# Chunk 0's gates ahead of the weight conversion, chunk 1's gates as a group, and filler products at a phase change, in a fused mLSTM and mixture-of-experts kernel

## Chip, core and metric

The kernel runs on one core of a Trainium2 chip. The metric is the device time in microseconds (us) of one execution; the runs before are given as the median of three. Five engines work side by side and meet through semaphores: PE multiplies matrices, ACT (ScalarE) evaluates functions and copies, DVE (VectorE) and POOL (GpSimd) do element-wise work, SP issues most transfers. Each engine takes its instructions in the order in which the program wrote them for it.

## What is computed

```
# 1. attention (mLSTM): 2 batches x 8 heads, 768 tokens, head size 40
for t in range(S):
    m_new = max(f_gate[t] + m, i_gate[t])
    f_stab, i_stab = exp(f_gate[t] + m - m_new), exp(i_gate[t] - m_new)
    C = f_stab * C + i_stab * outer(v_t, k_t);  n = f_stab * n + i_stab * k_t
    y[t] = sigmoid(o_gate[t]) * (C @ q_t) / max(abs(n . q_t), 1)
# 2. dense layer: 1536 tokens x 320, hidden 2048
x = softplus(x @ w_in) @ w_out
# 3. top-1 mixture: 8 experts, hidden 1024
e = argmax(x @ w_gate)
out = gate_w * sigmoid(x @ w_output_gate)[e] * (relu(x @ w1[e]) @ w2[e])
```

## The kernel before

The attention is done in 6 chunks (c) of 128 tokens for each of 2 batches (b). `gates` turns the gate inputs of some chunks into running sums: scans and small steps on DVE along the time axis (tiles mm, fg, acum, ig, scratch), transposes on PE (gps), exponentials on ACT and one negation on DVE (both into gts). Chunk 0 has a call of its own; chunks 1 to 5 share one, so their steps are 640 columns wide. A chunk then needs: the masked running sums on PE (ap), decays on ACT (abc<-ap, abc), scores on PE (sp), their product with the decays on DVE (abc<-sp,abc), the weighted values (pv), a state update (kv, cst), the part carried over from the chunk before (qc), and a division and sigmoid (num, sm, y, og). Its result is transposed (xp) and split into a high half (xh) and a rest (xl); where these two lie in the weights' tiles the trace names them win and wou.

The dense layer takes its weights from `w_in`, 16 pieces (n) that arrive as raw 64-bit words (wra); `conv` makes each a float (wta, three DVE steps), rounds it on ACT or DVE (win or wou) and subtracts the rounded part. Its products are ph (up), softplus on ACT and DVE (ab, g, gh, gl), and acc (down), in legs over ranges of pieces and blocks of 256 tokens.

Then the program passes to the experts. The last block's rows are routed (x2tp, lg, rsm, counts), the first four slots of tokens are put together on PE (xe), their halves written by ACT and DVE (flat<-xe), and the experts' products begin (ph<-w1s). `split_w2` rounds the eight experts' w2 on ACT (w2s<-w2raw) and `low_w2` subtracts the rounded part on POOL or DVE; the first down products (yp) wait for all eight. `warm` puts products of ones on PE that nothing reads.

The order of the work is set when the program is built. `Weaver` keeps a clock for each engine, prices every instruction (`Priced`), and always lets the task go on that can start earliest; the number given with `W.add` breaks ties. A `yield "V"` offers the next step to DVE (P is PE, A ACT, G POOL, S SP), a `yield [event]` holds the task back until the event has been signalled; these events steer only the order in which instructions are written down. The waits on the chip follow from the data. As every instruction is issued through one helper, the trace gives line 196 for nearly all of them, and tiles' names have to tell them apart.

Of the kernel before, what the change touches and what calls it, by code (L numbers as in the profile page):

```python
# [45 lines left out]
class Weaver:  # L46
# [4 lines left out]
    def __init__(self):  # L51
        self.clock = {e: 0.0 for e in "PAVGS"}
        self.tasks, self.cur, self.progress = [], None, 0.0
        self.last, self.at, self.dma = None, 0.0, 1.2
        self.columns = {}
        self.port = 0.0
        self.tick, self.hot = 0, False
# [92 lines left out]
class Priced:  # L150
# [3 lines left out]
    def __getattr__(self, name):  # L154
        fn = getattr(self.e, name)

        def call(*args, **kw):
# [19 lines left out]
            elif self.l == "V":  # L177
                wide = name in ("tensor_scalar", "tensor_copy", "memset") and not near and n not in (384, 768, 164)
                wide = wide or name == "tensor_scalar" and n in (384, 704)
                cost = 0.068 + n * (0.0065 if name == "reciprocal" else 0.00113 if "scan" in name else 0.00052 if wide  # L180
                                    else 0.00104)
                far = [t is None or t.space != PSUM for t in (src, kw.get("in1"))]
                port = all(far) and ("in1" in kw or wide)
            elif self.l == "G":
                port = not name.startswith("indirect") and n > 16
                cost = 1.04 if name.startswith("indirect") else 0.04 + n * 0.0008 if name in ("memset", "iota") else \
                    0.12 + n * (0.0033 if name == "tensor_copy" else 0.00092 if name == "affine_select" else
                                0.00175 if n in (320, 328, 164) else 0.0022)
            else:
                cost = 0.46  # L190
                run = 160 if out.shape[-1] == 40 else 512
                nbytes = out.shape[0] * n * 4 / (180e3 if run < 512 else 360e3)
# [42 lines left out]
def mlstm_moe_kernel(ctx: ExitStack, tc: tile.TileContext, q_t, k_t, k, v, i_gate, f_gate, o_gate,  # L235
# [72 lines left out]
    acum = moe.tile([GG, S], F32, tag="row1", name="acum")  # L308
    have_gates = Event(n=2)
    for r, t in x_ring.items():  # L310
        t.free[0] = (t.free[0][0], have_gates)
    read_acum, read_parts = Event(n=2), Event(n=2 + 2 * B * NSP)
    row_ring.free[0:3] = [(f"row{n}", ev) for n, ev in enumerate((have_gates, read_acum, read_parts))]
# [56 lines left out]

    gate_scan = Event()

    have_fi = Event()

    def load_gates():
        yield "S"
        SP.dma_start(fg, f_gate)
        SP.dma_start(ig, i_gate)
        W.signal(have_fi)

    def heat():
# [3 lines left out]
        for _ in range(HEAT):  # L385
            PE.matmul(warm, ones, ones.unsqueeze(1).to_broadcast([P, 2, P]), start=True, stop=True)
        W.signal(ev)

    def gates(n, c0, c1):
# [3 lines left out]
        if n:  # L393
            yield [gate_scan, have_g[0]]
        yield "V"
        DVE.tensor_tensor_scan(out=mm[:, t0:t1], data0=fg[:, t0:t1], data1=ig[:, t0:t1],
                               initial=NEG if n == 0 else mm[:, t0 - 1:t0], op0=ALU.add, op1=ALU.max)
        if n == 0:
            W.signal(gate_scan)
        yield "V"  # L400
# [140 lines left out]
    def chunk(b, c):  # L541
        if c > 1:
            yield [done_chunk[b][c - 2]]
        rank = 0 if c == 0 else 2 + 0.1 * c
        more = c < NCH - 1
# [77 lines left out]
        def carried():  # L623
            yield [done_c[b][c - 1], have_q[c]]
            box["num"] = num, _ = yield from work["num"].get([P, H, D1], F32, "num")
# [161 lines left out]
    def conv():  # L787
        for n in range(NF):
            W.cur.rank = RANKS[n]
            yield [have_raw[n]]  # L790
            raw, e1 = raws.pop(n)
# [111 lines left out]
    def route(blk, acc, full, part):  # L903
# [60 lines left out]
        for t in range(T2):  # L964
            ACT.activation(out=ex[:, t], in_=le[:, t], func=AF.Exp, bias=nmx[:, t:t + 1], accum_out=ssum[:, t:t + 1])
        ACT.activation(out=ef, in_=oge, func=AF.Exp, scale=-1.0)
        yield [Event(ranked), state[blk], have_rows]
        if final:
# [106 lines left out]

    have_room, up_done, have_turned = Event(), Event(), Event()
    have_last_lg, have_counts, have_chosen, have_parts, have_early = Event(), Event(), Event(), Event(n=TPB), Event()
# [301 lines left out]
    def split_w2(qn):  # L1379
# [5 lines left out]
        w2s = right["w2s"]  # L1385
        if qn == 0:
            yield [x_done]
        for e in range(E):
            yield [w2_raw[qn, e]] + ([begun[e + 2]] if qn == 0 else [])
            r, ev = w2_t.pop((qn, e))  # L1390
            yield "AV"
            copy(w2s[:, 0, :, e, :], r)
# [14 lines left out]
    def low_w2(qn, e, r, ev):  # L1407
        yield "VG"
        (psub if W.cur.on == "G" else vsub)(right["w2s"][:, 1, :, e, :], r, right["w2s"][:, 0, :, e, :].bitcast(F32))
# [6 lines left out]
    W.add(gates(0, 0, 1), 0)  # L1416
    W.add(gates(1, 1, NCH), 1)
    W.add(loads(0, 1), 1)
# [5 lines left out]
    for c in range(NCH):  # L1424
        for b in range(B):
            W.add(chunk(b, c), 0 if c == 0 else 2 + 0.1 * c)
    W.add(constants(), 5)
# [10 lines left out]
    def get_experts(s0, s1, ready, when):  # L1438
# [17 lines left out]
        evals.update(zip(range(s0, s1), vals))  # L1456
        W.signal(have_evals[s0])

    have_evals, have_meta = ({0: Event(), KNOWN: Event()} for _ in range(2))
# [10 lines left out]
    W.add(get_experts(KNOWN, NS, state[NBLK], rows_turned), 0)  # L1470
    W.add(turned_on(), 0)
    W.add(warm(turned_rows[0], 2), 0)
    W.add(warm(have_last_lg, 2), 0)
# [294 lines left out]
```

## Time and profile before

| what | value |
|---|---|
| median of three runs | 439.86 us (439.1 to 443.94) |
| profiled execution: device time / span from first to last instruction | 441.47 us / 439.8 us |
| PE busy / DVE busy / ACT busy / POOL busy, share of the span | 94% / 78% / 69% / 42% |
| mean granted TensorE clock | 0.97 of full speed |

The device time is 1.67 us over the span. A row of the timeline gives the start, the time busy, and in brackets how long the engine sat idle before it and what ended that. [...]

### The profile page before, as it was taken

Reading aid. Unit: us, or ns where it says so; the run is one execution under the profiler, and the core shown is the slowest. Engines: PE = TensorE matmul, PEld = TensorE weight load, DVE = VectorE, ACT = ScalarE, POOL = GpSimd, SP = SyncE. Lnnn points to the kernel's source line nnn. Section 1 sums busy time; section 2 is a strip of 40 time slices with the busy share of each in tenths; the row PEclk is TensorE's granted clock in tenths of the full one; section 3 lists DMA queues with packets and bytes.
Section 4 is the critical chain, followed back from the end, with each engine's and each line's share of the span. In section 5 each row is a group of like instructions: output and inputs, shape, how many; then the busy total and the mean of one; then the engine's idle time right before and its main releaser. Section 6 shows DMA issues by size and latency. Waiting matters only on the chain.

```text
span 439.8 us, 9798 instructions
## 1 busy us (share of the span) xinstructions
PE 414.8 (94%) x3073; PEld 394.0 (90%) x3073; DVE 344.0 (78%) x900; ACT 302.7 (69%) x877; POOL 182.7 (42%) x244
## 2 busy tenths in 40 slices
PE   8669999999999999999999999798999999999993
PEld 7657999999999999999999999677899898998893
DVE  3998999997998999997766656656954898798662
ACT  1559698978688887876967769417889675666230
POOL 5247585747120211130210102114766377387654
PEclk9896999999999999999999999969999999999998
DMA  8969659299347330132100101128636736644112
GB/s 266 334 199 305 207 150 279 91 299 318 132 121 290 107 103 30 32 91 60 38 11 28 38 1 38 57 87 254 204 124 179 253 105 221 202 133 147 41 66 78
DMA packets 32282, 62.88 MB, mean 143 GB/s; under 512 B 4218, under 2 KB 16765, under 8 KB 32230
## 3 DMA queue, kind: packets, MB, share of 16 engines
q1 hardware_dynamic: 30742, 57.87, 41.5%
q0 software_dynamic: 1488, 4.35, 2.7%
q8 instruction: 28, 0.46, 0.4%
q14 instruction: 24, 0.20, 0.2%
HBM read 54.05 MB, written 8.65 MB: 143 GB/s over the span
## 4 chain that ended last, share of the span: by engine, by line
PE 66%; DVE 11%; ACT 9%; DMA 8%; issue 3%; POOL 2%; SPq 1%; POOLq 0%; ACTq 0%; DVEq 0%
PE ph L196 26%; PE acc L196 17%; PE yp L196 11%; DMA out_dram<-yac,tki 3%; PE tp L196 2%; ACT abc L196 2%; PE lg L196 2%; DMA og<-in_o_gate_dram 2%; DVE wta L196 2%; PE sp L196 2%; DMA wra<-in_w_in_dram 2%; ACT ab L196 2%; PE pv L196 2%; DVE w2s L196 1%; DMA vn<-in_v_dram 1%
## 5 line engine op out<-in xcount | busy, mean ns | idle before, releaser
L196 ACT ACTIVATE ab<-ab 128x256 f32<-128x256 f32 x192 | 78.2, 416 | 2.9
L196 PE MATMUL ph<-w1s,flat 128*128 x312 | 59.6, 334 | 2.7 <-DVE hr L196 1.5
L196 POOL TENSOR_TENSOR w1s<-w1raw,w1s 64x256 fp32r<-64x256 f32 (+1 forms) x39 | 40.3, 1047 | 47.7 <-ACT w1s L196 23.9
L196 PE MATMUL acc<-win,gh 128*128 128x320 f32 x240 | 55.7, 317 | 0.0
L196 PE MATMUL yp<-w2s,hh 128*128 x240 | 54.5, 314 | 1.0 <-POOL w2s L196 0.9
L196 PEld LDWEIGHTS ph<-w1s,flat 128*128 128x128 f32 x312 | 46.6, 189 | 8.6 <-DVE hr L196 1.9
L196 DVE TENSOR_TENSOR gl<-g,gh 128x256 fp32r<-128x256 f32 x96 | 44.5, 467 | 12.3 <-ACT gh L196 11.2
L196 ACT ACTIVATE ab<-ph 128x256 f32<-128x256 f32 x96 | 36.3, 378 | 21.5 <-PE ph L196 20.9
L196 DVE SCALAR_TENSOR_TENSOR g<-ph,ab 128x256 f32<-128x256 f32 x96 | 39.9, 417 | 12.9 <-ACT ab L196 12.5
L196 POOL DMA_INDIRECT rows<-row,rsm x12 | 12.1, 1008 | 79.9 <-DVE rsm L196 25.9
L196 ACT CAST gh<-g 128x256 fp32r<-128x256 f32 x96 | 37.9, 397 | 8.9 <-DVE g L196 6.4
L196 POOL TENSOR_TENSOR w2s<-w2raw,w2s 128x640 fp32r<-128x640 f32 x20 | 35.8, 1811 | 17.3 <-ACT w2s L196 12.3
L196 PE MATMUL ph<-win 128*128 128x256 f32 x250 | 42.3, 289 | 0.0
L196 PEld LDWEIGHTS yp<-w2s,hh 128*128 128x128 f32 x240 | 39.7, 188 | 2.9 <-POOL w2s L196 1.1
L196 PEld LDWEIGHTS acc<-win,gh 128*128 128x128 f32 x240 | 38.7, 189 | 0.1
L196 DVE TENSOR_TENSOR hr<-ph,hr 128x256 f32<-128x256 f32 x60 | 24.5, 419 | 18.2 <-ACT hr L196 15.5
L196 PE MATMUL yp<-w2s,hl 128*128 x120 | 37.3, 311 | 0.0
L196 PE MATMUL acc<-win,gl 128*128 128x320 f32 x120 | 37.1, 309 | 0.0
L196 ACT COPY hr<-ph 128x256 f32<-128x256 f32 x60 | 22.8, 380 | 19.1 <-PE ph L196 18.5
L196 PEld LDWEIGHTS ph<-win 128*128 128x128 f32 x250 | 35.3, 193 | 0.0
L196 PE MATMUL acc<-wou,gh 128*128 128x320 f32 x144 | 33.2, 315 | 2.3 <-ACT gh L196 2.3
L196 ACT CAST w2s<-w2raw 128x640 fp32r<-128x640 f32 x32 | 23.3, 742 | 13.8 <-PE yp L196 13.8
(209 smaller groups left out, 1080.7 us busy)
## 6 DMA issues: line engine op xcount, KB each, us to landing
w1raw<-in_w_dram SPq DMA_DIRECT2D x32, 384.0 KB, 3.9
wra<-in_w_in_dram SPq DMA_DIRECT2D x16, 704.0 KB, 6.5
w2raw<-in_w_dram SPq DMA_DIRECT2D x32, 320.0 KB, 3.3
abc<-abc_dram SPq DMA_DIRECT2D x4, 1024.0 KB, 7.4
rows<-pad SPq DMA_DIRECT2D x19, 194.0 KB, 4.1
qT<-in_q_t_dram SPq DMA_DIRECT2D x6, 512.0 KB, 5.2
kn<-in_k_dram SPq DMA_DIRECT2D x5, 416.0 KB, 7.3
vn<-in_v_dram SPq DMA_DIRECT2D x6, 320.0 KB, 6.9
```

Source lines behind the costliest of these rows:

```text
L196: return fn(*args, **kw)
```

## The change

`conv` holds its first piece back until chunk 0's gates have been written down. The gates come as three groups: chunk 0, chunk 1, chunks 2 to 5. Chunk 1's attention gets rank 1.5 in place of 2.1, and its carried part waits, in the planner, for its gates. The planner's prices of a scan on DVE, of the first transfers and of the first products are altered. At the change of phase, five more products of ones are written behind the registers' load that follows the dense layer's last up product, the rounding of the first six w2 pieces is tied to the last block's exponentials (have_exps) and no longer to the first slots' halves (x_done), and in this first round rounding is offered to ACT alone and the subtraction to POOL alone.

```diff
@@ Weaver
-        self.last, self.at, self.dma = None, 0.0, 1.2
+        self.last, self.at, self.dma = None, 0.0, 2.4
@@ Priced
-                cost = 0.068 + n * (0.0065 if name == "reciprocal" else 0.00113 if "scan" in name else 0.00052 if wide
+                cost = 0.068 + n * (0.0065 if name == "reciprocal" else 0.0022 if "scan" in name else 0.00052 if wide
@@ load_gates, heat
         W.signal(have_fi)
+        W.dma += 0.9
...
+        W.clock["P"] = 8.1
         W.signal(ev)
@@ gates
         if n:
-            yield [gate_scan, have_g[0]]
+            yield [gate_scan[n - 1], have_g[n - 1]]
...
-        if n == 0:
-            W.signal(gate_scan)
+        if n < 2:
+            W.signal(gate_scan[n])
@@ chunk, carried
-        rank = 0 if c == 0 else 2 + 0.1 * c
+        rank = 0 if c == 0 else 1.5 if c == 1 else 2 + 0.1 * c
...
-            yield [done_c[b][c - 1], have_q[c]]
+            yield [done_c[b][c - 1], have_q[c], have_g[c]]
@@ conv
-            yield [have_raw[n]]
+            yield [have_raw[n]] + ([have_g[0]] if n == 0 else [])
@@ route
         ACT.activation(out=ef, in_=oge, func=AF.Exp, scale=-1.0)
+        if final:
+            W.signal(have_exps)
@@ split_w2
-        if qn == 0:
-            yield [x_done]
         for e in range(E):
-            yield [w2_raw[qn, e]] + ([begun[e + 2]] if qn == 0 else [])
+            yield [w2_raw[qn, e]] + ([have_exps if e < E - 2 else begun[e - 4]] if qn == 0 else [])
             r, ev = w2_t.pop((qn, e))
-            yield "AV"
+            yield "AV" if qn else "A"
@@ low_w2
-        yield "VG"
+        yield "VG" if qn else "G"
@@ the tasks
-    W.add(gates(1, 1, NCH), 1)
+    W.add(gates(1, 1, 2), 0.5)
+    W.add(gates(2, 2, NCH), 1)
...
-            W.add(chunk(b, c), 0 if c == 0 else 2 + 0.1 * c)
+            W.add(chunk(b, c), 0 if c == 0 else 1.5 if c == 1 else 2 + 0.1 * c)
@@ get_experts, the tasks
         W.signal(have_evals[s0])
+        if s0 == 0:
+            W.mark(known)
...
+    W.add(warm(known, 5), 0)
     W.add(warm(turned_rows[0], 2), 0)
```

What that moves on DVE, behind chunk 0's running sums (mm, fg, ig and acum are gates, wta<-wra the conversion of w_in, gts the negation that chunk 0's decays read). Before:

```order
L196 TENSOR_TENSOR ig<-ig,mm 80x128
L196 TENSOR_SCALAR wta<-wra 128x704
L196 TENSOR_SCALAR gts<-gps 128x16
L196 SCALAR_TENSOR_TENSOR wta<-wra,wta 128x704
L196 SCALAR_TENSOR_TENSOR mm<-fg,mm,ig 80x640
L196 SCALAR_TENSOR_TENSOR wta<-wra,wta 128x704
L196 TENSOR_TENSOR fg<-fg,mm 80x640
L196 TENSOR_TENSOR abc<-sp,abc 128x4x128 x2
```

After, the same place:

```order
L196 TENSOR_TENSOR ig<-ig,mm 80x128
L196 TENSOR_SCALAR gts<-gps 128x16
L196 SCALAR_TENSOR_TENSOR mm<-fg,mm,ig 80x128
L196 TENSOR_TENSOR fg<-fg,mm 80x128 x2
L196 TENSOR_SCALAR fg<-fg 80x128
L196 SCALAR_TENSOR_TENSOR acum<-scratch,fg 80x128
L196 CAST scratch<-acum 80x128
L196 TENSOR_SCALAR wta<-wra 128x704
L196 TENSOR_TENSOR scratch<-acum,scratch 80x128
L196 TENSOR_TENSOR abc<-sp,abc 128x4x128
```

The negation and chunk 1's running sums now stand ahead of the first conversion step; chunk 2 to 5's sums come some twenty rows later.

On PE, at the change of phase (TENSOR_LOAD reads the slots' experts into registers). Before:

```order
L196 MATMUL ph<-xl,wou 128x256 x3
L1452 TENSOR_LOAD pad
L196 MATMUL acc_4134<-wou,gh 128x320 x2
L196 MATMUL acc_4134<-wou,gl 128x320
L196 MATMUL acc_4180<-wou,gh 128x320 x2
L196 MATMUL acc_4180<-wou,gl 128x320
L196 MATMUL x2tp<-ident,row 128x128 x3
```

After:

```order
L196 MATMUL ph<-xl,wou 128x256 x3
L196 LDWEIGHTS ones
L1455 TENSOR_LOAD pad
L196 MATMUL warm<-ones 128x512
L196 MATMUL acc_4141<-wou,gh 128x320 x2
L196 MATMUL acc_4141<-wou,gl 128x320
L196 MATMUL acc_4177<-wou,gh 128x320 x2
L196 MATMUL acc_4177<-wou,gl 128x320
L196 MATMUL x2tp<-ident,row 128x128 x3
```

Five products of ones (one row shown of five, each with its load of weights) stand between the registers' load and the last down products.

On ACT, at the same place, from the last block's exponentials (rsm) on. Before:

```order
L196 ACTIVATE rsm<-lg,rsm 128x8 x2
L196 ACTIVATE rsm<-rsm 128x2
L196 CAST flat<-xe_4381 128x4x128
L196 CAST flat<-xe_4382 128x4x128
L196 CAST flat<-xe_4383 128x4x128
L196 COPY hr<-ph_4488 128x256
```

After:

```order
L196 ACTIVATE rsm<-lg,rsm 128x8 x2
L196 ACTIVATE rsm<-rsm 128x2
L196 CAST w2s<-w2raw 128x2x320 x6
L196 CAST flat<-xe_4396 128x4x128
L196 CAST flat<-xe_4397 128x4x128
L196 CAST flat<-xe_4398 128x4x128
```

Six of the eight w2 pieces are rounded ahead of the first slots' halves, where before the first came three rows behind them.

## Rows read from the trace of the kernel before

**Rows 1.** Windows: their length, busy time (instructions) of each engine, granted clock, DMA.
```profile
30.00:40.00 10.00, 7.17 (x35) 5.45 (x36) 9.71 (x16) 7.57 (x28) 7.20 (x9) 0.57 1.03 336
...
60.00:100.00 40.00, 39.97 (x345) 39.98 (x346) 37.91 (x82) 34.66 (x116) 25.90 (x36) 1.00 0.68 198
...
140.00:200.00 60.00, 60.00 (x464) 60.00 (x463) 58.21 (x123) 47.82 (x135) 11.22 (x14) 1.00 0.27 87
```
**Rows 2.** DVE's timeline, first 40 us: start, time busy, work, idle before it.
```profile
8.31 0.29 DVE L196 TENSOR_TENSOR ig<-ig,mm 80x128 f32<-80x128 f32 x1
11.84 0.53 DVE L196 TENSOR_SCALAR wta<-wra 128x704 uint32<-128x704 uint32 x1 [3.24 <-DMA wra<-in_w_in_dram]
...
38.22 0.55 DVE L196 TENSOR_TENSOR wou<-xp,win 128x384 fp32r<-128x384 f32 x1
```
**Rows 3.** ACT's timeline, first 40 us.
```profile
12.49 0.63 ACT L196 ACTIVATE abc<-ap,gts 128x128 f32<-128x128 f32 x2 [2.85 <-DVE gts L196]
...
32.99 0.47 ACT L196 ACTIVATE y<-og 128x320 f32<-128x320 f32 x1 [1.54 <-DMA og<-in_o_gate_dram]
```
**Rows 4.** DVE's groups from 8 to 60 us: count, busy us, mean ns, idle before.
```profile
L196 DVE SCALAR_TENSOR_TENSOR wta<-wra,wta 128x704 uint32<-128x704 uint32 x10 | 9.3, 930 | 0.1
L196 DVE TENSOR_TENSOR abc<-sp,abc 128x512 f32<-128x512 f32 x10 | 6.6, 674 | 0.0
L196 DVE TENSOR_TENSOR win<-wta,win 128x576 fp32r<-128x576 f32 x5 | 4.4, 888 | 2.1 <-ACT win L196 2.1
...
L196 DVE TENSOR_TENSOR fg<-fg,mm 80x640 f32<-80x640 f32 x2 | 2.2, 1080 | 0.0
L196 DVE SCALAR_TENSOR_TENSOR y<-og,y 128x320 f32<-128x320 f32 x4 | 1.8, 480 | 0.0
L196 DVE TENSOR_TENSOR_SCAN acum<-scratch,fg 80x128 f32<-80x128 f32 x5 | 1.8, 425 | 0.0
...
L196 DVE TENSOR_TENSOR_SCAN mm<-fg,mm,ig 80x640 f32<-80x640 f32 x1 | 1.5, 1541 | 0.0
```
**Rows 5.** The chain that ended last, its part from 39 to 50 us: start, length, what.
```profile
39.96 2.66 PE ph L196 x16
...
45.69 1.71 PE pv L196 x16
47.40 0.97 PE sp L196 x8
48.36 0.89 PE acc L196 x6
```
**Rows 6.** Waits at the change of phase: who for whom, us, times, longest.
```profile
PE acc L196 <- ACT gh L196: 2.3, 1, 2.3
...
PE ph L196 <- ACT w2s L196: 0.6, 1, 0.6
```
**Rows 7.** Windows of 1 us at the change of phase; the granted clock is third from the end.
```profile
284.00:285.00 1.00, 0.99 (x3) 0.26 (x2) 0.56 (x1) 1.00 (x4) 0.00 (x0) 0.50 0.21 23
...
294.00:295.00 1.00, 1.00 (x6) 0.83 (x5) 0.00 (x0) 0.00 (x0) 1.00 (x2) 0.93 0.53 199
```
**Rows 8.** The chain that ended last, its part at the change of phase.
```profile
285.65 2.38 PE lg L196 x12
...
289.17 0.85 PE warm L196 x2
...
291.94 2.13 PE warm L196 x5
...
321.30 1.75 PE yp L196 x12
```
**Rows 9.** ACT's timeline there.
```profile
295.13 0.59 ACT L196 CAST flat<-xe 128x512 fp32r<-128x512 f32 x1 [5.07 <-PE xe L196]
```
**Rows 10.** Groups of the whole span on ACT and POOL.
```profile
L196 POOL TENSOR_TENSOR w2s<-w2raw,w2s 128x640 fp32r<-128x640 f32 x20 | 35.8, 1811 | 17.3 <-ACT w2s L196 12.3 <-issue 4.9
...
L196 ACT CAST w2s<-w2raw 128x640 fp32r<-128x640 f32 x32 | 23.3, 742 | 13.8 <-PE yp L196 13.8
```

More of the change, by code (lines that the diff above doesn't have):

```diff
@@ L308, in mlstm_moe_kernel @@
     acum = moe.tile([GG, S], F32, tag="row1", name="acum")
-    have_gates = Event(n=2)
+    have_gates = Event(n=3)
     for r, t in x_ring.items():
         t.free[0] = (t.free[0][0], have_gates)
-    read_acum, read_parts = Event(n=2), Event(n=2 + 2 * B * NSP)
+    read_acum, read_parts = Event(n=3), Event(n=3 + 2 * B * NSP)
     row_ring.free[0:3] = [(f"row{n}", ev) for n, ev in enumerate((have_gates, read_acum, read_parts))]
@@ L369, in mlstm_moe_kernel @@
     nA, eA, eB = gts[:, 0], gts[:, 1], gts[:, 2]
-    gate_scan = Event()
+    gate_scan = events(2)
     have_fi = Event()
@@ L1074, in place_last @@
             W.signal(e)
-    have_room, up_done, have_turned = Event(), Event(), Event()
+    have_room, up_done, have_turned, have_exps, known = (Event() for _ in range(5))
     have_last_lg, have_counts, have_chosen, have_parts, have_early = Event(), Event(), Event(), Event(n=TPB), Event()
```

## The prediction

> **What bounds the kernel now.** I first cut the span into windows. From 60 us to the end of the dense layer PE has no idle time to speak of, and DVE follows it closely: 39.97 against 37.91 us of 40, then 60.00 against 58.21 of 60 [rows 1]. Time can therefore be won where PE is not at work at full clock, and that is at two places. The first is the start. From 30 to 40 us PE is idle for 2.83 of 10 us, its clock stands at 0.57 in the mean, and DVE is busy for 9.71 [rows 1]. The second is the change of phase near 280 us, where PE waits 2.3 us in one piece [rows 6] and then runs for ten microseconds at a clock of 0.50 [rows 7].
>
> The timelines show what ends the waits at the start. DVE has finished chunk 0's sums at 8.6 us and then stands still for 3.24 us, because the next instruction in its order is the first conversion step of w_in, whose transfer lands at 11.8 us. Behind that step stands the small negation that chunk 0's decays read [rows 2], and ACT, with those decays next in its order, is idle for 2.85 us until 12.49 us [rows 3]. From 11.84 us on DVE works almost without a break until the last half of chunk 0's result is written, at 38.77 us [rows 2], and only then are the dense layer's products behind it, from 39.96 us in the chain [rows 5].
>
> **Part 1, the gates.** With the negation ahead of the conversion, DVE can do it as soon as PE and ACT have turned the sums, some 0.6 us behind 8.6 us, so at about 9.2 us; ACT starts its decays near 9.4 instead of 12.49 us. The rest of DVE's gap up to 11.84 us takes in chunk 1's scan, its two additions, its limit and its running sum. They are 128 columns wide, and a fifth of the 640-column instructions and one of the five running sums make 0.31 + 2 x 0.22 + 0.43 = 1.2 us [rows 4]; with 0.1 us fixed for each it is under 2 us. They fit ahead of the transfer, so this part costs nothing; if the transfer landed 1 us earlier, that microsecond would be lost.
>
> For the stretch from 11.84 us I compare DVE's two lists, from the first conversion step to the last half of chunk 0's result. The new list has one first conversion step (0.53, rows 2), two of the further steps (0.93 each), one subtraction of a rounded weight (0.89) and one sigmoid step (0.48) less, and three score products of chunk 1 (0.67 each) more. Of the wide gates, a fifth of the scan and of two additions (0.31 + 0.43) and one running sum (0.43) have moved into the gap [rows 4]. The sum is -0.53 - 1.86 - 0.89 - 0.48 - 1.17 + 2.02 = -2.9 us. The additional group's fixed costs (five instructions, an estimate of 0.1 us each) take 0.3 back where they lie behind the gap, and the two short idle pieces of DVE in this stretch may go or stay. So the dense layer's first products begin **about 3 us earlier**, near 37 us. That is the bound from below, as far as DVE is the one that sets the pace.
>
> PE's list gives the bound from above. What stands ahead of the first up products now holds more: ten of chunk 1's sixteen score products (as many passes as 20 of the rows that take 0.97 us for 8, so 2.4 us), one batch's weighted values (1.71) and its state update (0.9, as half of them) [rows 5]. That is 5.0 us of PE's work done while it sat idle or ran at the low clock; there is room for it, since PE's idle time from 30 to 40 us alone is 2.83 us and the low clock there costs it about as much again [rows 1]. PE could so be 3 + 5 = 8 us ahead. Which of the two bounds holds is decided behind 60 us: a lead of PE over DVE is worth something only as far as DVE can follow, and it has 2.1 us to spare in the forty from 60 and 1.8 in the sixty from 140 [rows 1]. Farther on the two lists run side by side again: at the twentieth of the 96 up-and-down steps either kernel has the same products behind it. I take 3 us plus 2 us of DVE's slack, **5 us**, nearer to DVE's bound because its idle time in the last stretch is the smaller.
>
> What is queued behind the moved instructions: on SP, chunk 1's keys and queries now stand ahead of the fourth w_in piece, and the write of chunks 2 to 5's sums comes some 7 us later, with their broadcast behind it. The first consumer of that broadcast stands behind the first softplus pieces in the new order, so I count it at nothing; without that cover it is a wait of POOL and then ACT of 1 to 2 us. On ACT, chunk 1's sigmoid waits for its transfer as before (the engine was idle for 1.54 us there [rows 3]); behind it now stands a rounding of w_in and the first softplus, whose delay the range takes in.
>
> **Part 2, the products of ones.** PE's wait of 2.3 us for the last softplus ends at 281.88 us [rows 6]. Within it the registers are loaded, and then five products of 512 columns follow. On the chain five such products took 2.13 us at the low clock [rows 8], so at full clock half of that, 1.1 us: if the load takes no more than 1.2 us, they end before the data that PE waits for and cost nothing; if it takes the whole wait, 1.1 us. The clock stood at 1.00 up to the wait and 2 us behind its end, then at 0.50 until shortly behind 294 us [rows 7], though PE was busy all that time. With the gap half filled I take it that the clock stays up. Then the products on the chain take half: the logits 2.38 to 1.2 us, the two fillers ahead of the counts 0.85 to 0.4, the five ahead of the selection 2.13 to 1.1 [rows 8], in sum 2.7 us.
>
> **Part 3, w2's rounding.** Six roundings now stand on ACT ahead of the first slots' halves: 6 x 0.742 = 4.45 us [rows 10]. ACT was idle for 5.07 us there [rows 9], so with the old clock they are covered. With the clock up the halves are wanted 2.7 us earlier and ACT's exponentials end 1.6 us earlier (1.2 + 0.4, from above), so the cover is short by 2.7 - 1.6 - 0.6 = 0.5 us. What is won lies behind 300 us: six times 0.74 us leave ACT's queue where PE waited on ACT's w2 rounding (0.6, rows 6) and on ACT's and DVE's other steps that such pieces delayed. I take 1 us, between 0 and 2. All eight subtractions go to POOL: 8 x 1.811 = 14.5 us [rows 10] from about 295 us, some 20 small copies between them, so done near 314 us; the first products that need them begin at 321.3 us [rows 8], or 317 when all is earlier. That covers them. Parts 2 and 3 make 2.7 - 0.5 + 1 = **3.2 us**.
>
> **The sum.** 5 + 3.2 = 8.2 us off the profiled execution, 441.47 to 433.3 us (span 439.8 to 431.6). That execution lies 1.6 us over the median, so the same difference gives 439.86 - 8.2, near **431.7 us**.
>
> **The rivals.**
> B, the clock falls all the same. The trace speaks for it in that PE ran without a break from 281.88 us and the clock fell none the less at 284 us [rows 7], and the waits between the small products behind the gap stay. Then part 2 gives nothing, or costs up to 1.1 us, and part 3 its 1 us: 5 + 0.7 = 5.7 us, 434.2 us. [...]
> C, DVE eats the lead. The front gives 2.5 us, because conversion steps that were put off stand in the leg's way; with parts 2 and 3 the time is 434.2 us, without the clock 436.7 us.
> D, slower: the put-off conversion starves the first leg. In the new order the subtractions for weight pieces 2 and 3 come behind the second softplus rest, and PE, which has done its attention work ahead, has nothing to put in their place. If it is idle for some 3 us there and the low clock of the stretch from 30 to 40 us [rows 1] stays until 50, fourteen microseconds at half speed from the first products on cost 7 us. With the 8 us that PE had won, the front ends at -2, and if the fillers cost their 1.1 us and the clock falls as in B, nothing but part 3's 1 us stands against it: 442 us. It decides if the granted clock is still 0.50 beyond 46 us. Against it speaks that DVE works without a break ahead of that point in either order, and reaches it earlier.
>
> **How the numbers follow.** Chances: forecast 0.52, B 0.24, C 0.16, D 0.08. The range runs from both upper bounds that I think can come together (the front's 8 us, 4.5 us behind: 427.0) to C without the clock (437), with a little more for what an order of other instructions does in 200 us of closely packed work: 426.5 to 437.5 us. A measurement of this kernel tells about 1%, 4.4 us, from no change, so faster begins below 435.5 us: nearly all of the forecast, two thirds of B and half of C, 0.75. Within 1%: 0.19. Slower, over 444.3 us: 0.06, since D's price lies inside the 1% and its tail reaches beyond.
>
> **What would show it.** In the new profile ACT's first decays start near 9.4 us, DVE's gap ahead of the first conversion step is under 1 us, and the first up products stand near 35 to 37 us with most of chunk 1's scores behind them. PE's clock is up again before 42 us. At the change of phase the five products lie inside the wait of the last down products, and the windows behind it show 1.00; six roundings of w2 end before the first slots' halves, and the first yp comes some 3 us closer to the last acc. The prediction is wrong if the lead at 60 us is gone at 200 us (then DVE set the pace), if the windows still show 0.50 behind the gap (B), or if yp waits for POOL.

## The result and the profile after

The changed kernel takes 434.79 us in the median of four runs (433.88 to 435.17); the kernel before, beside it, 441.72 (439.1 to 443.94). The ratio is 0.9876, 95% interval 0.9835 to 0.9916; a second measurement on another chip gave 433.79 against 440.38 us, 0.9848 (0.9816 to 0.9881). It is faster by 1.2 to 1.5%. The prediction was 431.7 us with a range of 426.5 to 437.5.

The profiled execution after the change took 435.17 us (span 433.5) where the one before took 441.47 (439.8): 6.3 us off. Two points split that. The last pair of down products (the acc behind PE's longest wait) starts at 281.88 us before and at 280.05 after, so **the front brought 1.83 us**. From that point to the first yp it took 39.25 us before and 34.87 after, so **the change of phase brought 4.4 us**. Behind the first yp the two are alike (118.7 and 118.6 us to the end).

Windows of the kernel after (length, busy time and instructions of PE, PE's weight load, DVE, ACT, POOL; granted clock, DMA share, GB/s); they answer to [rows 1]:

```profile
30.00:40.00 10.00, 8.99 (x78) 8.40 (x79) 10.00 (x20) 6.00 (x20) 4.25 (x5) 1.00 0.61 178
40.00:50.00 10.00, 7.83 (x55) 7.71 (x54) 9.84 (x21) 7.62 (x26) 9.26 (x24) 0.83 0.87 276
50.00:60.00 10.00, 8.88 (x77) 8.70 (x75) 7.30 (x16) 8.18 (x26) 4.45 (x9) 1.00 0.91 251
60.00:100.00 40.00, 40.00 (x345) 40.00 (x344) 36.88 (x82) 37.90 (x124) 25.21 (x39) 1.00 0.79 253
100.00:140.00 40.00, 37.99 (x304) 36.97 (x303) 37.63 (x83) 28.98 (x84) 10.88 (x15) 1.00 0.49 166
140.00:200.00 60.00, 60.00 (x464) 60.00 (x463) 58.85 (x123) 47.96 (x139) 10.27 (x15) 1.00 0.26 89
```

The stretch from 30 to 40 us is cured: PE is busy for 8.99 of 10 at full clock (7.17 at 0.57 before). But PE now stands still in places where it did not before: 2.17 us from 40 to 50 with a clock of 0.83, 1.12 from 50 to 60, and 2.01 from 100 to 140 (before: 0, 0.29 and 0.30). There the lead went.

The start, on DVE and then ACT (start, time busy, work, idle before it), answering to [rows 2, 3]:

```profile
9.66 0.17 DVE L196 TENSOR_SCALAR gts<-gps 128x16 f32<-128x16 f32 x1 [1.04 <-ACT gts L196]
...
10.26 1.51 DVE L196 TENSOR_TENSOR fg<-fg,mm 80x128 f32<-80x128 f32 x2
...
12.66 0.52 DVE L196 TENSOR_SCALAR wta<-wra 128x704 uint32<-128x704 uint32 x1
...
36.98 0.54 DVE L196 TENSOR_TENSOR wou<-xp,win 128x384 fp32r<-128x384 f32 x1
```

```profile
9.99 0.62 ACT L196 ACTIVATE abc<-ap,gts 128x128 f32<-128x128 f32 x2
```

DVE's gap shrank from 3.24 to 1.04 us and ACT's decays start at 9.99 instead of 12.49 us. But chunk 1's steps do not fit into the rest of the gap: they hold DVE from 9.76 us until the first conversion step at 12.66, which is 0.82 us later than before. The two additions alone take 1.51 us. The last half of chunk 0's result ends at 37.52 us, 1.25 earlier (2.9 were forecast).

What stands ahead of PE's first longer wait, on PE and then POOL:

```profile
37.22 0.84 PE L196 MATMUL ph<-win 128*128 128x256 f32 x5
...
43.26 1.47 PE L196 MATMUL kv<-v,kn 128*104 128x82 f32 x8 [2.17 <-POOL v L196]
44.45 0.88 PE L196 MATMUL acc<-win,gh 128*128 128x320 f32 x2
```

```profile
39.27 0.66 POOL L196 MEMSET tri<- 128x128 bf16 x1
40.00 1.21 POOL L196 TENSOR_SCALAR_AFFINE_SELECT tri<-tri 128x128 bf16<-128x128 bf16 x1
...
42.36 0.13 POOL L196 IOTA rem<- 128x1 f32 x1
42.46 0.74 POOL L196 TENSOR_TENSOR v<-v,sm 128x328 f32<-128x328 f32 x1
```

PE waits 2.17 us for a product on POOL, and on POOL the fifteen constants (tri to rem, 39.27 to 42.49 us) stand ahead of it. Behind this wait the clock falls to 0.50, from about 43.5 to 46.9 us.

At 107 us, ACT and then the queue of SP:

```profile
107.65 0.47 ACT L196 ACTIVATE y<-og 128x320 f32<-128x320 f32 x1 [1.36 <-DMA og<-in_o_gate_dram]
```

```profile
90.18 8.79 SPq L196 DMA_DIRECT2D rows<-pad  x14
99.07 1.05 SPq L196 DMA_DIRECT2D kT<-in_k_t_dram  x2
100.17 2.54 SPq L196 DMA_DIRECT2D rows<-pad  x5
102.82 0.41 SPq L196 DMA_DIRECT2D og<-in_o_gate_dram  x1
```

The load of o_gate stands behind nineteen stores of 194 KB each (3.7 MB) that lay out the rows, and ACT waits 1.36 us for it. DVE's g waits for ACT's ab behind that (1.43), and PE three times for DVE (0.55, 0.41 and 0.59 us from 109 to 115). Before, ACT waited 0.96 us for the same load until 112.36 us, where PE had other products in its order.

The change of phase on PE, answering to [rows 8]:

```profile
277.63 1.26 PE L196 MATMUL warm<-ones 128*128 128x512 bf16 x5
280.05 0.57 PE L196 MATMUL acc<-wou,gh 128*128 128x320 f32 x2 [1.17 <-ACT gh L196]
...
283.29 0.74 PE L196 MATMUL lg<-wg,x2T 128*128 128x16 f32 x6
284.38 0.84 PE L196 MATMUL lg<-wg,x2T 128*128 128x16 f32 x6 [0.35 <-DVE x2T L196]
...
285.82 1.00 PE L196 MATMUL warm<-ones 128*128 128x512 bf16 x2
...
288.53 1.61 PE L196 MATMUL warm<-ones 128*128 128x512 bf16 x5
289.80 3.16 PE L196 MATMUL xe<-S,part 128*128 128x512 f32 x12
```

The five products lie inside the wait and cost nothing; the logits run at a granted clock of 1.00. The windows of 1 us, answering to [rows 7], show that the clock then fell after all, from about 286 to 289 us instead of 284 to 294:

```profile
284.00:285.00 1.00, 0.65 (x7) 0.62 (x7) 0.33 (x1) 0.00 (x0) 0.00 (x0) 1.00 0.67 247
286.00:287.00 1.00, 1.00 (x8) 0.54 (x7) 0.63 (x6) 0.45 (x4) 0.00 (x0) 0.50 0.00 0
...
294.00:295.00 1.00, 1.00 (x7) 0.96 (x7) 0.35 (x2) 0.00 (x0) 1.00 (x2) 1.00 0.34 41
```

w2's work there, on ACT (answering to [rows 9]) and on POOL:

```profile
287.15 3.85 ACT L196 CAST w2s<-w2raw 128x640 fp32r<-128x640 f32 x6
291.11 0.59 ACT L196 CAST flat<-xe 128x512 fp32r<-128x512 f32 x1
```

```profile
307.73 1.57 POOL L196 TENSOR_TENSOR w2s<-w2raw,w2s 128x640 fp32r<-128x640 f32 x1
```

ACT goes from the six roundings straight to the halves, and POOL's last subtraction ends at 309.3 us, over five before the first yp at 314.92. From 300 to 320 us PE is busy for 20.00 of 20, against 17.89 before.

### The profile page after: what moved, and what is told of

Same layout as the page of the kernel before. It is cut to its first block, busy times and chain, and to the rows that moved or that the text cites. A ratio compares the mean times of both kernels' runs of the same rounds, so it can differ in the third digit from the quotient of the medians.

```text
span 433.5 us, 9833 instructions
## 1 busy us (share of the span) xinstructions
PE 410.1 (95%) x3078; PEld 390.5 (90%) x3078; DVE 343.5 (79%) x904; ACT 302.5 (70%) x879; POOL 181.0 (42%) x246
## 5 line engine op out<-in xcount | busy, mean ns | idle before, releaser
L196 POOL TENSOR_TENSOR w1s<-w1raw,w1s 64x256 fp32r<-64x256 f32 (+1 forms) x39 | 39.4, 1027 | 48.5 <-ACT w1s L196 25.0
L196 DVE TENSOR_TENSOR gl<-g,gh 128x256 fp32r<-128x256 f32 x96 | 42.5, 447 | 7.9 <-ACT gh L196 7.2
L196 POOL TENSOR_TENSOR w2s<-w2raw,w2s 128x640 fp32r<-128x640 f32 x22 | 39.1, 1808 | 8.7 <-issue 4.9
L196 PE MATMUL ph<-win 128*128 128x256 f32 x250 | 40.8, 286 | 0.0
L196 PEld LDWEIGHTS ph<-win 128*128 128x128 f32 x250 | 34.3, 190 | 0.0
```

What stands on the lines that cost most here:

```text
L196: return fn(*args, **kw)
```

## The experiments

All of them but the second start from the changed kernel. For each the text gives the ratio to the kernel before on the same chip with its 95% interval, and from the profiled execution two durations: from the last acc group to xe<-S, which goes with the clock (8.75 us with nine products of ones, where it stays at 1.00, and 11.50 with none, where it is at 0.50 for over 10 us), and from there to the first yp, where w2's work lies. Before: 11.63 and 27.62 us. After: 9.75 and 25.12.

**The front alone.** The transition is as it was before.

```diff
-    W.add(warm(known, 5), 0)
# split_w2, low_w2 as before: x_done, begun[e + 2], "AV", "VG"
```

> The changed kernel with the transition put back: no five products of ones, w2's roundings behind x_done on either engine. Its weave up to the end of the dense layer is the changed kernel's. Theory (the front kept only 1.8 us of its lead, the transition gave 4.4): the last acc group of the down products starts near 280 us as in the changed kernel, and the time is 4.4 us above the changed kernel's 434.8, so near 439.2 (ratio to before 0.994 to 0.997). Rival (the front carries the gain and the transition little): 435 to 436.5 (0.986 to 0.989).

Measured: 436.56 us, ratio 0.9919 (0.9893 to 0.9945). By the time, the front is worth 0.8%. But the profiled execution (434.68 us, one of the shortest of twelve, 433.36 to 438.91) shows a lead quite unlike the changed kernel's, with the same order of the front, and here PE's wait is 0.62 us:

```profile
41.20 0.96 PE L196 MATMUL kv<-v,kn 128*104 128x82 f32 x8 [0.62 <-POOL v L196]
...
275.57 0.56 PE L196 MATMUL acc<-wou,gh 128*128 128x320 f32 x2 [2.26 <-ACT gh L196]
```

The last acc group starts at 275.57 us, 6.3 ahead of before. My theory, that the front always keeps 1.8 us, fell here. The change of phase took 11.42 and 27.89 us, as before.

**The transition alone**, in the kernel before.

```diff
+    W.add(warm(known, 5), 0)
# split_w2, low_w2 as after: have_exps, "A", "G"
```

> The kernel before with the transition alone: five products of ones once the experts are known, six w2 roundings on ACT ahead of flat, the low halves on POOL. Theory (front and transition add up): the front as before, first ph near 39.6 us, last acc at 281.9; first yp about 35 us behind that; 437.3 us (0.988 to 0.992). Rival (the transition's gain needs the front's lead, because the down products end with nothing in hand): 440 to 441.7 (0.996 to 1.0).

Measured: 437.96 us, ratio 0.9958 (0.9935 to 0.9982). The last acc group starts at 281.71 us, 0.2 from before; 10.98 and 25.43 us follow, 2.8 us less than before, where the changed kernel's profile had 4.4 less. So the transition brings a part without the front. The ratio lies at the edge of the rival's range and outside the theory's, so the part is smaller than forecast; by the medians the two parts add up (0.8 and 0.4% to the 1.2% of the first measurement), but the intervals would also allow other sums.

**Without the products of ones.**

```diff
-    W.add(warm(known, 5), 0)
```

> The changed kernel without the five products of ones alone. Theory (they held the clock for the logits and fillers): the granted clock falls to 0.50 near 283 to 284 as in the kernel before, the logits' group takes 2.4 us and the fillers 0.85 and 2.1, xe starts 2 to 3 us later; 437 to 437.5 us (2.2 to 2.7 above the changed kernel). Rival (the transition's 4.4 us is all the moved w2 work): the time within 0.7 us of the changed kernel's 434.8, since w2's roundings on ACT and its low halves on POOL end no earlier and the first slots wait for those.

Measured: 434.59 us, ratio 0.9882 (0.9848 to 0.9916), no more than the changed kernel. The time alone would speak for the rival. The profile tells otherwise:

```profile
277.31 0.56 PE L196 MATMUL acc<-wou,gh 128*128 128x320 f32 x2 [2.26 <-ACT gh L196]
288.81 3.23 PE L196 MATMUL xe<-S,part 128*128 128x512 f32 x12
314.01 0.45 PE L196 MATMUL yp<-w2s,hh 128*128 x2
```

11.50 and 25.20 us: the clock's part is lost entirely, w2's is kept. This execution had a front that was 2.7 us better, which covers the loss; whether the other five had it too, their times alone don't show. The time cannot resolve it, the two stretches can.

**The products of ones alone.**

```diff
-            yield [w2_raw[qn, e]] + ([have_exps if e < E - 2 else begun[e - 4]] if qn == 0 else [])
+            yield [w2_raw[qn, e]] + ([begun[e + 2]] if qn == 0 else [])
# and x_done, "AV", "VG" as before
```

> The changed kernel with w2's first pass put back (roundings behind x_done on ACT or DVE, low halves on DVE or POOL) and the five products of ones kept. From the last acc group's start to the first yp it took 39.3 us with neither edit, 36.7 with w2's alone, 34.3 to 35.1 with both. Theory (the two add up): 37.0 to 37.7 with the products of ones alone, 436 to 437.3 us (ratio 0.990 to 0.993). Rival (the clock gives nothing so long as the first slots wait for w2's low halves on POOL): 38.8 to 39.4, 438 to 439 us.

Measured: 435.59 us, ratio 0.9874 (0.983 to 0.9918). 8.76 and 27.84 us, 36.6 in sum: the clock's part is kept, w2's is lost. With neither edit the sum is 39.3, with w2's alone 36.7, with both 34.3 to 35.1 in eight profiles (36.4 in the transition alone). The theory's 37.0 to 37.7 and its 436 us were a little too long, the rival's 38.8 fell.

**Nine products of ones.**

```diff
-    W.add(warm(known, 5), 0)
+    W.add(warm(known, 9), 0)
```

> The changed kernel with nine products of ones in place of five, in the wait before the last down products. In the changed kernel the granted clock was 1.00 to 285.9 us, then 0.50 to 289.9; with none it fell near 279.5, 2 us before the logits. Theory (how full PE was before the logits decides how long the clock stays up): with nine it stays at 1.00 some 2 to 4 us longer, xe and the fillers at 286 to 290 run at full clock; 1 to 1.5 us off from the last acc group to the first yp (34.9 to 33.5), 433.3 to 434 us. Rival (the fall comes from the small products of the logits and counts themselves): clock as in the changed kernel, first yp 34.9 us behind the last acc group, 434.5 to 435.3.

Measured: 434.58 us, ratio 0.9875 (0.9845 to 0.9904). The clock stayed at 1.00:

```profile
280.00:290.00 10.00, 8.71 (x57) 6.17 (x57) 6.75 (x35) 5.69 (x16) 1.04 (x2) 1.00 0.25 82
```

The stretches are 8.75 and 25.56 us. But it also stayed up with five products in four other profiles (the products of ones alone, one group without rank, constants in the idle stretch, scans one row later), and fell in six, to 0.50 for 3.4 us in five of them and for 6.8 in the transition alone. So four more products are not what decides it, and the time is the rival's. In the three profiles without any it stood at 0.50 for over 10 us (twice what the windows' means lack of 1.00; in the run without the products of ones from 278.7 us, not from 279.5 as the expectation has it). When the clock stays up, only some 0.4 us more is won to the first yp, because PE then waits 1.16 to 1.21 us for DVE's pad (in three profiles) instead of 0.65.

**One group for chunks 1 to 5, no rank for chunk 1.**

```diff
-    W.add(gates(1, 1, 2), 0.5)
-    W.add(gates(2, 2, NCH), 1)
+    W.add(gates(1, 1, NCH), 1)
...
-        rank = 0 if c == 0 else 1.5 if c == 1 else 2 + 0.1 * c
+        rank = 0 if c == 0 else 2 + 0.1 * c
# and the same rank where chunk's tasks are added
```

> The changed kernel with chunks 1 to 5 in one group of gates again and without the rank 1.5 for chunk 1; conv's wait and the new prices (queue start, scans, heater) stay, and the transition stays. Chunk 0's negation still stands ahead of w_in's first step on DVE. Theory (the early start of chunk 0 is worth about 2 us of DVE, and chunk 1's scores ahead of the up products are worth the rest): chunk 0's decays near 9.5 us, the up products start earlier than before but with less of the attention done, the lead at the last acc group is 1.5 to 2.5 us, 435.5 to 436.5 us. Rival A (chunk 1 alone makes the lead): lead under 0.5, time as with the transition alone, 437.5 to 438.5. Rival B (the own group with its 22 smaller DVE instructions eats what the rank gives): as the changed kernel or below it, 433.5 to 435.

Measured: 439.2 us, ratio 0.9978 (0.9954 to 1.0003), no faster than the transition alone:

```profile
65.97 0.86 PE L196 MATMUL ph<-win 128*128 128x256 f32 x5 [1.78 <-ACT win L196]
...
285.69 0.56 PE L196 MATMUL acc<-wou,gh 128*128 128x320 f32 x2 [1.17 <-ACT gh L196]
```

The up products start at 31.84 us, 7.8 ahead of before, at the low clock (0.83 in the mean from 20 to 40 us; three products took 0.84 us at 33.06 and 0.52 at 34.50), and then the weights are missing: PE waits 1.78 us for a rounded piece at 66. From 60 to 140 us PE is idle for 3.30 us, against 0.33 before, and the last acc group comes 3.8 us later than before. The starved leg is what rival D told of; its low clock is not: it is 0.83 in the mean from 40 to 50 us, an ap product of the form that took 0.63 us at 31.02 takes 0.38 at 44.77, and from 50 us on the clock is 1.00. The theory, 2 us for the early start by itself, fell.

**The group kept, the rank left out.**

```diff
-        rank = 0 if c == 0 else 1.5 if c == 1 else 2 + 0.1 * c
+        rank = 0 if c == 0 else 2 + 0.1 * c
# and the same rank where chunk's tasks are added
```

> The changed kernel with chunk 1's gates in their own group, but its attention not ranked first (2.1 again in place of 1.5). Without group and rank it took 439.2 us and the last acc group started at 285.69. Theory (that chunk 1's attention is put first is what makes the front's lead): 437.5 to 439.5 us, last acc group at 283 to 286, the up products start earlier (32 to 35 us) and more of the attention stands behind them. Rival (it is chunk 1's gates being there early): 433.5 to 435.5 us, last acc group at 277 to 280.5.

Measured: 434.75 us, ratio 0.987 (0.983 to 0.991), as the changed kernel. By the time the theory fell and the rival held: chunk 1's gates in a group of their own carry the front, 4.4 us between the medians of this kernel and the last one; the rank adds nothing that shows in the time. The down products end in another order here, so the point to compare is the turning of the last block's rows behind them (the first x2tp): 282.81 us, 4.3 earlier than in the last kernel, 1.3 later than in the changed kernel's first profile. What the group is worth without the early start of chunk 0 was not run. (Conv's wait for chunk 0's gates does nothing beside the new prices: without it the order on all engines is the same. With the old prices it is what puts the negation ahead. Both are read from the order as written, not from runs.)

**POOL's constants nine rows later**, on POOL alone.

```diff
         yield "G"
+        emit_constants(Priced(W, Quiet(), "G"))   # priced here, nothing written
...
+        yield 3.0
+        yield "G"
+        emit_constants(nc.gpsimd)
```

> The changed kernel with POOL's fifteen constants (tri, iota, pad, ... 3.1 us at 39.27 to 42.46) issued nine POOL instructions later; the order on all other engines is the changed kernel's. Theory (these constants stand ahead of the v product that kv waits 2.17 us for, and the idle PE behind it drops the clock to 0.50 from 43.8 to 47): the wait falls below 0.5 us, the clock stays at 1.00 there, the first acc starts 1.5 to 2 us earlier, and most of 2 to 3 us is still there at the end: 432 to 433 us. Rival (DVE at 37.6 of 40 between 100 and 140 takes any lead away): the first acc is earlier all the same, but the last down acc starts within 0.5 us of 280.05, and the time is 434.3 to 435.3.

Measured: 435.27 us, ratio 0.9894 (0.9849 to 0.9939); last acc group at 281.07 us. The wait at 41 us was gone and the first acc started at 42.06 instead of 44.45, as the theory had it. But the constants, now at 50.55 to 52.4 us, stand ahead of the next product of the same kind. They make 1.9 of the 3.83 us that PE waited for it, and PE lost more than had been won:

```profile
53.81 0.97 PE L196 MATMUL kv<-v,kn 128*104 128x82 f32 x8 [3.83 <-POOL v L196]
```

**The constants in POOL's idle stretch** at 55 to 59 us: the same edit with `yield 5.0`.

> The changed kernel with POOL's fifteen constants put into POOL's idle stretch near 55 to 59 us (behind the two y products there, 16 rows later); every other engine's order is the changed kernel's. In the run with them nine rows later, the wait of kv for POOL's v was gone at 41 us and a wait of 3.83 us stood at 53.8, again behind the constants. Theory (the constants' 2 to 3 us on POOL are what takes the front's lead): neither wait is there, the clock stays at 1.00 from 40 to 60, the first acc starts near 42 us, the last acc group of the down products at 276 to 277.5, and the time is 430.5 to 432.5 us. Rival (DVE, busy without a gap from 20 to 50, sets the pace there and POOL's order only shows it): another wait takes the place (sp or pv for DVE's abc or num), the last acc group starts at 279 to 281, 434 to 435.5 us.

Measured: 433.18 us, ratio 0.983 (0.980 to 0.9861), last acc group at 280.07. Neither long wait is there (kv's longest is 0.97 us). This time the clock fell earlier, behind an idle stretch of PE at 29 to 31 us (clock third from the end):

```profile
30.00:31.00 1.00, 0.18 (x2) 0.00 (x0) 1.00 (x3) 0.90 (x4) 0.00 (x0) 1.00 0.00 0
34.00:35.00 1.00, 1.00 (x6) 1.00 (x6) 1.00 (x3) 0.00 (x0) 1.00 (x1) 0.50 0.67 154
39.00:40.00 1.00, 1.00 (x6) 1.00 (x6) 1.00 (x3) 1.00 (x4) 0.14 (x1) 0.50 1.15 281
```

At half clock the first up products moved to 39.51 us, and at 107 us PE waited all the same. The last acc group is where the rival had it, though what took the lead was the low clock and the wait behind o_gate, and the time lies between the two forecasts.

**DVE's scans of chunks 2 to 5 one row later**, behind the product that PE waits for at 30 us, on DVE alone.

```diff
...
+        scans(DVE if n < 2 else Priced(W, Quiet(), "V"))
...
         yield "V"
+        if n == 2:
+            scans(nc.vector)
```

> The changed kernel with the four scans of chunks 2 to 5 (acum x4, 3.04 to 3.07 us on DVE beside POOL's work, 2.55 in the two executions with a large lead) one row later on DVE, behind the next abc product that PE's pv waits for; all other engines' order is the changed kernel's. Theory (two things take the lead: PE's idle time at 30 to 32 us behind these scans, and kv's wait behind POOL's constants): PE is busy over 1.8 of 30 to 32 (1.15 in the changed kernel), but kv still waits 1.5 to 2.2 us, the clock may still fall behind that, last acc group at 278.5 to 280.5, 433.3 to 434.8 us. Rival (DVE's sum sets the pace, so its order there changes nothing): PE idle at another place before 41 us, same last acc group and time as the changed kernel's. Other rival (the scans' place is all): last acc group at 275 to 277.5 and 430.5 to 432.5 us with the constants where they were.

Measured: 433.18 us, ratio 0.9837 (0.979 to 0.9884). The last acc group starts at 278.61 us, PE is busy for 1.65 of the two microseconds from 30, and kv still waits 2.18 us: close to the theory's numbers, with PE less busy and the time 0.1 us shorter than it said.

**Both together.**

```diff
# the constants at yield 5.0, and the scans one row later
```

> The changed kernel with both: POOL's constants in its idle stretch near 55 to 59 us, and DVE's four scans one row later. With the constants moved alone (433.2 us) the clock fell in its profiled execution at 33.8 to 40.2 us, behind PE's idle time at 29 to 31, and the lead went there instead. Theory (with both gone nothing lets PE idle before 60 us): clock 1.00 from 20 to 60, no wait of kv for POOL's v over 1 us, first acc near 41.5 to 42.5, last acc group at 275 to 277.5, 429.5 to 431.5 us (ratio 0.975 to 0.980). Rival (a larger lead ends in front of DVE at 107 to 116 us, where sp waited 0.55 to 1.28 us for DVE's cst): these waits grow past 2.5 us, last acc group at 279 to 280.5, 432.7 to 434 us.

Measured: 433.13 us, ratio 0.9833 (0.9789 to 0.9877), last acc group at 279.48. Until 60 us it is nearly as the theory has it: clock 1.00 from 20 us on, no wait of kv for POOL's v, first acc at 41.45. Then the lead ends at 107 us, on PE and ACT:

```profile
109.03 0.71 PE L196 MATMUL sp<-qT,kT 104*128 104x128 f32 x4 [2.30 <-DVE cst L196]
```

```profile
107.09 0.47 ACT L196 ACTIVATE y<-og 128x320 f32<-128x320 f32 x1 [3.12 <-DMA og<-in_o_gate_dram]
```

So the rival was right about the place. It was wrong about the cause: DVE is late because ACT is, and ACT waits 3.12 us for o_gate.

**The changed kernel once more.**

> The changed kernel itself once more, beside the three others of this chip. So far the same order of the front gave a last acc group at 280.05, 275.6 and 277.31 us in three profiled executions. Theory (the front's lead differs from execution to execution by what POOL and DVE do to one another at 27 to 45 us, and does not wear off later): the time lies between 432.5 and 435.5 us, and the wait of kv for POOL's v near 41 us and the last acc group go together: 2 us of wait with 280, 0.6 us with 276 to 277.5. Rival (the front always keeps 1.8 us, and the other two executions differ by their transition's edits): last acc group at 279.5 to 280.5 with any wait.

Measured: 433.79 us, ratio 0.9848 (0.9816 to 0.9881); last acc group at 280.37 with a kv wait of 2.17, ACT's wait for o_gate 1.87. Both the theory's pair and the rival's range fit this, so it does not decide. Elsewhere the pair does not hold: with the products of ones alone PE did not wait for POOL's v near 41 us and the group started at 280.10, behind 10.2 us at half clock.

**ACT's wait for o_gate and PE's time.** Ten profiles share the changed kernel's order of the front on PE, ACT and SP. In all of them PE is busy without a break from 60 to 100 us and again from 140 to 200. What it loses between 100 and 140, beside ACT's wait:

| kernel | ACT's wait for o_gate | PE idle, 100 to 140 us |
|---|---|---|
| front alone | none | 1.04 |
| products of ones alone; scans later | 0.40; 0.40 | 1.28; 1.28 |
| nine products | 0.64 | 1.45 |
| constants nine rows later | 1.11 | 1.77 |
| after, its first profile | 1.36 | 2.01 |
| without the products of ones | 1.44 | 2.10 |
| after, once more | 1.87 | 2.52 |
| constants in the idle stretch | 2.09 | 2.75 |
| both | 3.12 | 3.77 |

From a wait of 1.1 us up, PE loses the wait and 0.65 us, to a hundredth. A larger lead does not by itself mean a longer wait. ACT came to this step earliest in the front alone, and did not wait:

```profile
99.30 0.39 SPq L196 DMA_DIRECT2D og<-in_o_gate_dram  x1
```

```profile
103.17 0.47 ACT L196 ACTIVATE y<-og 128x320 f32<-128x320 f32 x1
```

With both edits it came 0.8 us later, at 103.97, and waited longest. In all ten the load was issued only 2.5 to 3.9 us before ACT wanted it, and where ACT waited, 3.84 us (scans later) to 6.08 us (both) passed from the issue to the wait's end. By and large the long waits go with the long times there; why these differ is open. That the nineteen stores ahead of the load make it late was not tried by moving them; it is read from the queue's order.

None of the three kernels with the lowest medians (433.13 and twice 433.18 us) can be told apart from the changed kernel by its interval; both edits together (433.13 us) are the lowest median, and beat the kernel before by 1.7%.

## Why the prediction was nearly right

**The total** lies 3.1 us above the forecast (2.1 in the second measurement) and inside the range. In the profiled execution 8.2 us were forecast and 6.3 came, with the front too large by 3.2 and the change of phase too small by 1.2. That the two errors pull against each other is luck. (The sum behind the range's lower end makes 427.4, not 427.0; the range holds either.)

**The front (forecast 5, came 1.83 in that execution; 0.8 to 6.3 in the ten profiles of its order, four of them with rows of POOL or DVE moved).** The start went much as told: the gap on DVE, the decays near 10 us, the clock up from 30 us on, the first up products at 37.22. Chunk 1's steps in the gap cost 0.82 us where nothing had been counted for them (the 0.1 us fixed for an instruction was an estimate that [rows 4] bear out: a scan of 128 columns took 0.425 us there, 0.12 over a fifth of the 1.541 of 640 columns), and DVE's list behind them became shorter by 2.1 us, where 2.9 had been added up. The first acc came 3.7 us earlier, 44.45 in the timeline after; before it was

```profile
48.12 0.54 PE L196 MATMUL acc<-win,gh 128*128 128x320 f32 x2
```

The step that failed is the choice of DVE's slack as what decides behind 60 us. PE did not lose its lead by DVE's sum: DVE is busy for 36.88 of 40 from 60 us, with PE at 40.00. It lost it at single places that I had passed over: POOL's constants ahead of kv's product with 3.4 us of low clock behind, and o_gate's load. (PE's idle time gives an estimate: 1.83 us at the end and 1.7 more idle from 100 to 140 than before make a lead of 3.5 us at 100, and half of it was gone by 140, so the sign that I had named for DVE's pace came half true for another reason. DVE has a share in it: in the front alone, where ACT does not wait, 0.58 of PE's 1.04 us of idle time there is a wait for DVE's num.) In the part on what is queued I counted SP at nothing, with only the sums' broadcast in view; the attention's other loads, and the stores ahead of them, stand in the same queue. In the run with both edits the microseconds won at the first place went at the second; in the front alone, with 0.62 us at the first, ACT did not wait at the second and the lead of 6.3 us stayed. So the one does not have to follow from the other. Why two executions of the same order had a lead 2.7 and 4.5 us larger is not settled; in both, DVE reached the scans at 26.80 and 27.07 us, not at 27.44 to 27.84 as in the six others with the scans in their place, and did the four in 2.55 and 2.56 instead of 3.04 to 3.07 us, and in both the clock stayed at 1.00 up to 60 us.

**The bound from PE's list, chunk 1's work ahead.** Right in kind, but not through the rank: its gates being there early is enough.

**Rival D** came in part where chunk 1 has no group of its own: 3.8 us late at the last acc group, by a starved leg and not by its low clock. In the changed kernel the low clock came back at 43.5 and left at 46.9, just past the point from which I had said it decides, but PE's lead by then was larger than the price (3.7 us at the first acc; 3.4 us at a clock of 0.50 cost 1.7 by an estimate from the clock's two values).

**Part 2 (forecast 2.7).** To xe<-S it took 9.75 instead of 11.63 us, so 1.9, and 2.5 to 2.9 where the clock stayed up. Rival B came half true: the clock fell in six of eleven profiles with products of ones, for 3.4 microseconds instead of ten in most of them. Its price was wrong, since about half of what a clock that stays up gives there is taken back by the wait for DVE's pad. In those six profiles it falls among the small products behind the filled gap. PE's short waits there are much alike with the clock falling and staying up (0.36 and 0.35 us after, the same with the products of ones alone), so the traces do not show that they decide it.

**Part 3 (forecast 1 less 0.5 for the cover).** 25.12 us instead of 27.62, so 2.5; with w2's edit the stretch is 24.8 to 26.0 us in all profiles, without it 27.6 to 27.9. The term was mis-sized on both sides. The halves are not late, because PE waits for DVE's pad (0.65 us, as long with the old rounding) and not for them. And not one wait went but four: before, PE waited 0.55, 0.55, 0.60 and 0.42 us from 303 to 317 us for ACT's and DVE's flat, w2s and hl; after, 0.42 once. The rest of the 2.5 us lies in PE's busy time, 24.05 instead of 25.42 us for nearly the same products, and is not traced further.

## What to carry to other kernels

A lead that is won early can be lost at the next thing that comes late; list those before counting the lead: loads that stand behind large stores in the same queue and are issued just before they are needed (here o_gate's, issued 2.5 to 3.9 us ahead, with ACT waiting up to 3.12 us), and small set-up work that the planner put "where there was room" on another engine (here POOL's constants, ahead of a wait of 2.17 us). When times can't resolve two edits, cut the profile at points that both kernels pass and compare the pieces: here execution to execution the front varied by 5 us, and the pieces behind it by a few tenths as long as the clock did the same. An edit in several parts wants each part left out once: the part named first in the change (the rank, conv's wait) may do nothing that shows, and the unspectacular one (a group of its own) most of it.

## What was unexpected of the hardware

**The same instruction on POOL took about four times as long in one profile as in another.** POOL's tri took 0.66 and 1.21 us in the changed kernel's profile and 0.20 and 0.29 us in that of the front alone:

```profile
38.20 0.20 POOL L196 MEMSET tri<- 128x128 bf16 x1
38.48 0.29 POOL L196 TENSOR_SCALAR_AFFINE_SELECT tri<-tri 128x128 bf16<-128x128 bf16 x1
```

In the longer case the first ended at 39.93 us, 0.15 behind a conversion step of DVE (39.27 to 39.78), and the second at 41.21, 0.15 behind DVE's next (40.18 to 41.06). On DVE's side five scans took 1.82 us before, with POOL idle but for the first 0.3, and four took 3.04 to 3.07 beside four POOL products. In the first of these cases the ends follow one another by 0.15 us; what ties them together no row here shows. From 20 to 50 us, where DVE is busy for 29.80 of 30 us in the changed kernel, steps of both lists were longer side by side (the two of tri, and the scans at 0.76 us each instead of 0.36), but they need not be: in the front alone DVE was at abc<-sp,abc (38.09 to 38.77 us) beside the same two, and neither was long.

**Behind the same short idle time of PE the clock fell in two profiles and stayed up in a third.** With PE almost idle from 30 to 31 us (0.01, 0.18 and 0.00 us busy) the clock stayed at 1.00 up to 43 us in the changed kernel's second profile, fell from 33.5 to 40.3 us with the constants in the idle stretch, and from 31.5 to 41.8 with the products of ones alone:

```profile
34.00:35.00 1.00, 1.00 (x11) 1.00 (x11) 1.00 (x3) 0.00 (x0) 1.00 (x1) 1.00 0.73 154
```

```profile
34.00:35.00 1.00, 1.00 (x9) 0.96 (x9) 0.47 (x1) 0.29 (x2) 1.00 (x1) 0.50 0.75 159
```

The first row is of the changed kernel once more, the second of the products of ones alone. PE is busy throughout in both. Up to the fall the two have the same order on PE and all but the same waits (0.70 and 1.17 us from 28 to 31 us in the first, 0.71 and 1.16 in the second). What decides between them the rows don't show.
